# A planned transformer block on one core: the last quarter of the queries in two jobs, pooled PSUM banks, b2 on GpSimd, LN2's transposes by DMA

## The chip, the cores and the metric

The kernel runs on one core of one Trainium2 chip. A core has five engines with one in-order instruction queue each: TensorE (PE, matmuls), VectorE (DVE), ScalarE (ACT), GpSimd (POOL) and SyncE (SP, which here issues all DMAs). They wait for each other through semaphores. SBUF holds the working data, PSUM (eight banks of 128 x 512 fp32) what PE writes. The metric is the time of one execution on the device in microseconds (us), median of several runs.

## The reference

One pre-LN transformer block on 2048 tokens of width 1024, in bfloat16: 32 heads of 32 channels, full softmax attention, feed-forward width 3584, tanh GELU.

```python
q, k, v = qkv(x_norm @ wqkv)                       # x_norm = layernorm(x), 32 heads of 32
p = softmax(q @ k.T * 32 ** -0.5)                  # per head, 2048 x 2048
h = x + (p @ v) @ wo
out = h + gelu(layernorm(h) @ w1 + b1) @ w2 + b2   # (1024, 3584), (3584, 1024)
```

## The kernel before

**Attention.** The 2048 queries are handled in four chunks of 512 (`NCH`). A chunk runs through 16 pairs of heads (`p16`); for each pair eight rounds follow (`attention_round`). A round scores two blocks of 128 keys for two heads: four matmuls on four row groups of the array (`Att.qk`, L634), each 32 x 128 weights by 512 queries, into two "units" of two PSUM banks (three units, banks 0 to 5, take turns). ACT turns each unit into probabilities with one exp of 128 x 1024 elements (L643, 1024 of them in all). `pv_unit` (L654, L658) then accumulates values and row sums of one key block into bank 6, four narrow matmuls of 32 columns of weights side by side. After the last key block `finish` copies sums and values out (L666, L668), takes reciprocals (L673) and multiplies into `OT` (L680, in pieces of 128 queries for the very last pair, L677).

**Background.** PE has time left beside attention, and a list of "bg" tasks fills it, all through bank 7. Beside chunk 0 these are the rest of the q, k, v projections; beside chunk 1 to 3 the feed-forward part of the chunk before: `wo` (projection, x added by DVE, L719), `ln2`, `ffn1` and `ffn2`, with `late_q` (queries of a later chunk) between the second and third tile of LN2 for the first two of them. In the background a matmul of 128 columns of weights is given as four narrow ones on four column groups (`mm`, L439); four narrow matmuls of 512 columns take as long as one full one and are called a unit here. A group is what one bank takes: 8 units for wo, ffn1 and a late projection, 29 for ffn2, the first of them `two_row` times `b2t`, which adds twice b2 (the evacuation L782 halves the bank and adds h).

`ln2` takes statistics of a tile of 128 tokens on DVE, inverse roots on POOL (L492 to L498), normalises on DVE (L502), transposes eight 128 x 128 blocks on PE (L508) and copies the bank into `hnT` (L514 by DVE, L512 by ACT in the last chunk). `ffn1` adds b1 on the way out of PSUM (L748 by DVE, L751 by ACT in the last chunk), and GELU is x^2 (L754), a cubic (L756), tanh on ACT (L758) and a product (L760) into `gT`.

**The tail.** After chunk 3's attention nothing is left to run beside its own feed-forward part. It uses full matmuls (L443), all eight banks in turn, and a second set of ring buffers (`R2`) in the space of the keys and values. The weights come in blocks of 512 KB: w1 and wo through a ring of four slots (`w1r`), w2 through seven (`w2r`); two of w2's slots share their place with `hnT`, two with the late queries' input.

**The order.** Nothing is ordered at run time. `Graph.add` notes what each task reads and writes, and `Graph.schedule` simulates the five engines with fixed costs and writes one order per engine: PE takes qk first, pv when five are waiting (`PV_FORCE`) or no bg task is ready, else the earliest bg task (`pick_pe`); the other engines take the ready task of least `prio`, then the earliest. A bg task that needs bank 7 depends on the last reader of that bank. Semaphore waits are worked out from this order afterwards. At the very start PE runs 80 matmuls on `b2t` and `ident` (L798) when it has nothing else.

Of the kernel before, what the change touches and what calls it, by code (L numbers as in the profile page):

```python
# [27 lines left out]
class Task:  # L28
    __slots__ = ("eng", "fns", "occ", "lat", "deps", "prio", "kind", "mode", "left", "succ", "ready", "done",
                 "order", "inc", "flow", "value", "lane", "waits", "bytes", "hold")  # L30

    def __init__(self, eng, fns, occ, lat, prio, kind, mode):
# [14 lines left out]
        self.hold = None  # L47


class Graph:  # L50
# [7 lines left out]
    def __init__(self, n_lanes):  # L58
        self.tasks = []
        self.regions = {}  # L60
        self.n_lanes = n_lanes

# [35 lines left out]
    def schedule(self, pick_pe, switch=0.1, dma_rate=280.0, dma_lat=2.1, dma_issue=0.06):  # L98
# [13 lines left out]

        def release(t):
            t.ready = max([d.done - (d.lat if d.eng == t.eng == E.PE else 0.0) for d in t.deps], default=0.0)
            heapq.heappush(upcoming[t.eng], (t.ready, num[t], t))
            heapq.heappush(events, t.ready)
# [5 lines left out]
        while n < total:  # L122
# [5 lines left out]
            for e in self.ENGS:  # L128
                while free[e] <= now + 1e-9:
# [18 lines left out]
                    rd.remove(t)  # L148
                    start = now
                    if e == E.PE:  # L150
                        if state["mode"] != t.mode:
                            start += switch
                        state["mode"] = t.mode
# [16 lines left out]
                    heapq.heappush(events, free[e])  # L170
                    n += 1
                    for s in t.succ:
                        s.left -= 1
                        if s.left == 0:
                            release(s)
# [109 lines left out]
def build_kernel(nc, A_x, A_wqkv, A_wo, B_w1, B_b1, B_w2, B_b2, out):  # L285
# [51 lines left out]
    two_row, B_two = sb(top, "two_row", [P, P], BF)  # L337
# [91 lines left out]
    def pe(fns, occ, reads=(), writes=(), kind="bg", mode="full", prio=0, after=()):  # L429
        return gr.add(E.PE, fns, occ, 0.16, reads, writes, prio, kind, mode, after)  # L430

    def mm(bank, lhsT, rhs, start, stop, reads, narrow, cols=(0, 512)):
# [3 lines left out]
        if narrow:  # L436
            fns = []
            for j in range(4):
                fns.append(lambda p, j=j: p.matmul(psum[32 * j:32 * j + 32, bank, c0:c1], lhsT[:, 32 * j:32 * j + 32], rhs,  # L439
                                                   start=start, stop=stop, tile_position=(0, 32 * j), skip_group_check=True))  # L440
            pe(fns, occ, reads=reads, writes=[B_ps[bank]], mode="col")
        else:
            pe(lambda p: p.matmul(psum[:, bank, c0:c1], lhsT, rhs, start=start, stop=stop),  # L443
               occ, reads=reads, writes=[B_ps[bank]], mode="full")
# [18 lines left out]

    pool(lambda g: g.memset(ident[:], 0.0), 0.3, writes=[B_ident])
# [6 lines left out]
    pool(lambda g: g.memset(two_row[:], 0.0), 0.3, writes=[B_two])  # L471
    pool(lambda g: g.memset(two_row[0:1, :], 2.0), 0.3, reads=[B_two], writes=[B_two])
    pool(lambda g: g.memset(b2t[:], 0.0), 1.0, writes=[B_b2t])
# [32 lines left out]
    def transposes(src_ap, B_src, bank, dst_ap, B_dst, evac, prio):  # L506
        for dc in range(DC):
            pe(lambda p, dc=dc: p.transpose(psb[:, bank, dc * P:(dc + 1) * P], src_ap[:, dc * P:(dc + 1) * P], ident[:]),  # L508
               0.064, reads=[B_src, B_ident], writes=[B_ps[bank]], prio=prio)
        src = psb[:, bank, :].rearrange("p (dc t) -> p dc t", dc=DC)  # L510
        if evac == "act":
            act(lambda a: a.activation(dst_ap, src, ACT.Copy), 1024, reads=[B_ps[bank]], writes=[B_dst], prio=-1)  # L512
        else:
            dve(lambda v: v.tensor_copy(dst_ap, src), c_dve_ps(1024), reads=[B_ps[bank]], writes=[B_dst])  # L514

# [19 lines left out]
    def proj(which, g, tc, bank, evac, direct=False):  # L535

        blk, c = divmod(which * D + g * P, 512)
        for dc in range(DC):
            mm(bank, Wall[:, blk, dc, c:c + P], xnT[:, tc, dc, :], dc == 0, dc == DC - 1,
# [3 lines left out]
        if evac == "act":  # L543
            act(lambda a: a.activation(stg[:, s, :], psum[:, bank, :], ACT.Copy), 512,
                reads=[B_ps[bank]], writes=[B_stg[s]], prio=-1)
        else:
            dve(lambda v: v.tensor_copy(stg[:, s, :], psum[:, bank, :]), c_dve_ps(512), reads=[B_ps[bank]], writes=[B_stg[s]])  # L547
# [28 lines left out]
    def late_q(R, qc, gs):  # L576

        dma(R.xq[:, :, :], xd[qc - 1], P * 8192, reads=[B_xd[qc - 1]], writes=[R.B_xq], prio=0)
        for g2 in range(gs // 2, G // 2):
            s = wblock(R, A_wqkv[:, 256 * g2:256 * g2 + 256], 0)  # L580
            for k in range(2):
                g = 2 * g2 + k
                for dc in range(DC):
                    mm(7, R.w1[:, s, dc, k * P:k * P + P], R.xq[:, dc, :], dc == 0, dc == DC - 1,
                       [R.B_w1[s], R.B_xq], True)
                o = R.next("os", R.nos)
                dve(lambda v, o=o: v.tensor_copy(R.ost[:, o, :], psum[:, 7, :]), c_dve_ps(512),
                    reads=[B_ps[7]], writes=[R.B_ost[o]])
                dma(qd[g, qc], R.ost[:, o, :], P * 1024, reads=[R.B_ost[o]], writes=[B_qd[g][qc]], prio=0)

    def proj_v(tt, q, bank, evac):

        blk, c = divmod(256 * q, 512)
        blk += 4
        for k in range(2):
            tc, t4 = divmod(tt + k, 4)
            for dc in range(DC):
                mm(bank, xnT[:, tc, dc, t4 * P:(t4 + 1) * P], Wall[:, blk, dc, c:c + 256], dc == 0, dc == DC - 1,
                   B_W[blk][c // P:c // P + 2] + [B_xnTt[tc][t4]], True, cols=(256 * k, 256 * k + 256))
        dst = V[:, tt:tt + 2, 256 * q:256 * q + 256]  # L600
        src = psum[:, bank, :].rearrange("p (t c) -> p t c", t=2)
        wr = [B_V[4 * (tt + k) + q] for k in range(2)]
        if evac == "act":
            act(lambda a: a.activation(dst, src, ACT.Copy), 512, reads=[B_ps[bank]], writes=wr, prio=-1)
        else:
            dve(lambda v: v.tensor_copy(dst, src), c_dve_ps(512), reads=[B_ps[bank]], writes=wr)  # L606


    class Att:
# [9 lines left out]
        def qk(self, qc, units):  # L619

            fns, banks, rd, us = [], [], [], []
            for p16, kt in units:
                tc, k4 = divmod(kt, 4)
                half, i = divmod(k4, 2)
# [5 lines left out]
                for j in range(2):  # L630
                    r0 = 64 * half + 32 * j

                    def fn(p, j=j, r0=r0, u=u, p16=p16, tc=tc, i=i, qs=qs, pr=pr):
# [373 lines left out]
```

## Time and profile before

| | |
|---|---|
| median of 3 runs | 1203.92 us (1203.0 to 1205.25) |
| profiled execution, first to last instruction | 1417.9 us |
| mean granted TensorE clock in the profiled execution | 0.749 of full speed |
| busy PE / ACT / DVE / POOL | 1366.2 / 1085.3 / 673.2 / 37.9 us |
| 1024 exps (L643) | 989.2 us busy, 1025 ns each |
| last exp ends / last matmul ends | 1255.0 / 1415.0 us |

The profile is of one execution, which was longer than the timed ones; its page gives busy time by engine, its chain follows the work that ended last back from the end, its groups give the mean time of one instruction by line of the code, and its stages give busy time, granted clock and DMA use within a stretch. A busy PE counts pipelined matmuls, whose ends are modelled.

### The profile page before, as it was taken

What the parts mean: (1) busy time and instruction counts of PE and PEld (TensorE: products, weight loads), DVE (VectorE), ACT (ScalarE), POOL (GpSimd) and SP (SyncE); (2) the same over time, 40 slices, a digit from 0 to 9 for tenths busy, and PEclk for the clock granted to TensorE, in tenths of its full rate; (3) what the DMA queues carried; (4) which work ended last, traced back from release to release, by engine and by line L of the source; (5) the groups of instructions that cost most, each with busy time, mean ns of one, the idle gap of its engine ahead of it and who ended that gap; (6) DMA issues with size and microseconds to landing.
All of it is one profiled execution on the core that took longest, in us unless ns stands there. A gap on an engine that the chain in (4) does not pass through costs nothing.

```text
span 1417.9 us, 37847 instructions
## 1 busy us (share of the span) xinstructions
PE 1366.2 (96%) x17326; PEld 510.9 (36%) x17336; DVE 673.2 (47%) x1165; ACT 1085.3 (77%) x1189; POOL 37.9 (3%) x96
## 2 busy tenths in 40 slices
PE   8999999999999999999999999999999999978999
PEld 5544443433333333332333333333333333324333
DVE  7354444443546774223547762225677612245710
ACT  4778787878888888888888888888988888844500
POOL 2000000000100000000100000000000000001000
PEclk7777777777777777777777777777777777766777
DMA  6800000025343222303342230422323322202222
GB/s 165 224 2 13 28 13 14 13 72 156 101 122 101 76 69 72 124 16 98 107 124 71 83 98 16 124 71 63 107 73 98 102 66 85 87 0 75 74 93 71
DMA packets 165793, 112.29 MB, mean 79 GB/s; under 512 B 25345, under 2 KB 162817, under 8 KB 164866
## 3 DMA queue, kind: packets, MB, share of 16 engines
q1 hardware_dynamic: 165634, 109.87, 26.2%
q8 instruction: 136, 2.23, 0.7%
q14 instruction: 23, 0.19, 0.1%
HBM read 98.58 MB, written 11.27 MB: 77 GB/s over the span
## 4 chain that ended last, share of the span: by engine, by line
PE 91%; ACT 4%; DVE 3%; issue 1%; POOL 1%; DMA 0%; POOLq 0%; DVEq 0%
PE ps L439 48%; PE ps L654 17%; PE ps L634 12%; PE ps L443 10%; ACT PT L643 3%; PE ps L658 2%; PE ps L798 1%; ACT xnT L512 1%; DVE a_xh L748 1%; PE ps L508 1%; DVE V L606 0%; DVE stg L547 0%; DVE Osb L668 0%; DVE Dsb L666 0%; DMA a_w1r<-in_A_wqkv_dram 0%
## 5 line engine op out<-in xcount | busy, mean ns | idle before, releaser
L643 ACT ACTIVATE PT<-ps 128x1024 bf16<-128x1024 f32 x1024 | 989.2, 1025 | 180.5 <-PE ps L634 166.1
L654 PE MATMUL ps<-PT,V 128*32 128x512 bf16 x2048 | 383.4, 457 | 13.7 <-DVE V L606 6.2
L658 PE MATMUL ps<-PT,ones 128*32 128x512 bf16 x2048 | 384.8, 458 | 0.0
L439 PE MATMUL ps<-a_w2r,gT 128*32 128x512 bf16 x2688 | 241.9, 452 | 0.0
L634 PE MATMUL ps<-QT,KT 32*128 32x512 bf16 x2048 | 216.7, 414 | 7.4 <-ACT PT L643 7.3
L439 PE MATMUL ps<-a_hnT,a_w1r 128*32 128x512 bf16 x2688 | 215.2, 454 | 4.0 <-DVE a_xh L748 3.2
L654 PEld LDWEIGHTS ps<-PT,V 128*32 128x32 bf16 x2048 | 103.3, 104 | 143.9 <-issue 89.3
L634 PEld LDWEIGHTS ps<-QT,KT 32*128 32x128 bf16 x2048 | 51.5, 91 | 272.3 <-ACT PT L643 164.5
L439 PE MATMUL ps<-xnT,Wall 128*32 128x512 bf16 x1344 | 111.6, 453 | 7.0 <-ACT xnT L512 4.8
L439 PEld LDWEIGHTS ps<-a_w2r,gT 128*32 128x32 bf16 x2688 | 77.3, 109 | 112.0 <-issue 103.3
L673 DVE RECIPROCAL Dsb<-Dsb 128x128 f32<-128x128 f32 x128 | 115.1, 928 | 1.0
L439 PEld LDWEIGHTS ps<-a_hnT,a_w1r 128*32 128x32 bf16 x2688 | 70.6, 107 | 108.0 <-issue 71.4
L782 DVE SCALAR_TENSOR_TENSOR a_ost<-ps,hch 128x512 bf16<-128x512 f32 x24 | 16.6, 692 | 189.8 <-PE ps L439 189.7
L658 PEld LDWEIGHTS ps<-PT,ones 128*32 128x32 bf16 x2048 | 103.5, 104 | 6.6 <-issue 6.6
L748 DVE TENSOR_SCALAR a_xh<-ps,b1f 128x512 bf16<-128x512 f32 x84 | 63.1, 751 | 81.3 <-PE ps L439 80.2
L666 DVE COPY Dsb<-ps 64x512 f32<-64x512 f32 x64 | 44.4, 694 | 101.5 <-PE ps L658 100.1
L439 PE MATMUL ps<-Wall,xnT 128*32 128x256 bf16 x2048 | 83.8, 314 | 0.0
L547 DVE CAST stg<-ps 128x512 bf16<-128x512 f32 x40 | 27.5, 689 | 89.2 <-PE ps L439 89.2
L443 PE MATMUL ps<-a_hnT,b_w1r 128*128 128x512 bf16 x219 | 64.5, 470 | 2.1 <-ACT a_hnT L512 1.5
L439 PEld LDWEIGHTS ps<-Wall,xnT 128*32 128x32 bf16 x2048 | 57.6, 107 | 22.7 <-issue 11.3
L443 PE MATMUL ps<-a_w2r,gT 128*128 128x512 bf16 x219 | 64.1, 461 | 0.5
L439 PE MATMUL ps<-a_w1r,OT 128*32 128x512 bf16 x768 | 63.1, 453 | 0.8 <-DVE hch L719 0.5
(69 smaller groups left out, 875.5 us busy)
## 6 DMA issues: line engine op xcount, KB each, us to landing
a_w2r<-in_B_w_dram SPq DMA_DIRECT2D x56, 512.0 KB, 4.6
a_w1r<-in_B_w_dram SPq DMA_DIRECT2D x42, 512.0 KB, 3.9
a_w1r<-in_A_wo_dram SPq DMA_DIRECT2D x16, 512.0 KB, 4.7
QT<-q_scratch SPq DMA_DIRECT2D x60, 128.0 KB, 2.8
b_w1r<-in_B_w_dram SPq DMA_DIRECT2D x14, 512.0 KB, 3.8
a_w1r<-in_A_wqkv_dram SPq DMA_DIRECT2D x11, 512.0 KB, 5.1
xrb<-in_A_x_dram SPq DMA_DIRECT2D x16, 256.0 KB, 3.9
Wall<-in_A_wqkv_dram SPq DMA_DIRECT2D x16, 256.0 KB, 5.4
```

Source lines behind the costliest of these rows:

```text
L439: fns.append(lambda p, j=j: p.matmul(psum[32 * j:32 * j + 32, bank, c0:c1], lhsT[:, 32 * j:32 * j + 32], rhs, start=start, stop=stop, tile ...
L443: pe(lambda p: p.matmul(psum[:, bank, c0:c1], lhsT, rhs, start=start, stop=stop), occ, reads=reads, writes=[B_ps[bank]], mode="full")
L508: pe(lambda p, dc=dc: p.transpose(psb[:, bank, dc * P:(dc + 1) * P], src_ap[:, dc * P:(dc + 1) * P], ident[:]), 0.064, reads=[B_src, B_ide ...
L547: dve(lambda v: v.tensor_copy(stg[:, s, :], psum[:, bank, :]), c_dve_ps(512), reads=[B_ps[bank]], writes=[B_stg[s]])
L634: return p.matmul(psum[:, 2 * u + j, :], KT2[r0:r0 + 32, p16, tc, i, :], QT2[r0:r0 + 32, qs, pr, :], start=True, stop=True, tile_position= ...
L643: act(lambda a, u=u, s=s: a.activation(PT[:, s, :, :], psum[:, 2 * u:2 * u + 2, :], ACT.Exp, bias=0.0, scale=SCALE), 1024, reads=[B_ps[2 * ...
L654: fns.append(lambda p, j=j, h=h: p.matmul(psum[32 * j:32 * j + 32, bank, :], V[:, kt, 32 * h:32 * h + 32], PT[:, s, j, :], start=first, st ...
L658: fns.append(lambda p, j=j: p.matmul(psum[64 + 32 * j:96 + 32 * j, bank, :], ones32[:, :], PT[:, s, j, :], start=first, stop=last, tile_po ...
L666: dve(lambda v: v.tensor_copy(Dsb[64 * pr:64 * pr + 64, :], psum[64:128, bank, :]), c_dve_ps(512), reads=[B_ps[bank]], writes=B_Dsb[pr], p ...
L673: dve(lambda v, k=k: v.reciprocal(Dsb[:, 128 * k:128 * k + 128], Dsb[:, 128 * k:128 * k + 128]), 0.93, reads=[B_Dsb[0][k], B_Dsb[1][k]], w ...
L748: dve(lambda v, i=i, fc=fc, bank=bank: v.tensor_scalar(R.xh[:, i, :], psum[:, bank, :], b1f[:, fc:fc + 1], None, ALU.add), c_dve_ps(512), ...
L782: dve(lambda v, o=o, t4=t4, j=j, bank=bank: v.scalar_tensor_tensor(R.ost[:, o, :], psum[:, bank, :], 0.5, hch[:, t4, 512 * j:512 * j + 512 ...
```

## The change

Five things change. (1) Chunk 3 becomes two jobs of 256 queries. A unit of scores then holds two key blocks of 256 queries for two heads, so the exps stay 1024 of 128 x 1024, and qk, pv and ffn1 issue twice as many matmuls of half the width. The feed-forward part of the first half is a background job of its own, that of the second half the tail. (2) A bank is no longer written into a task: tasks form a `Group`, which gets a bank from a pool when its first matmul is picked. The pool holds bank 7, and banks 0 to 6 join as attention ends. A group may be picked when it is the earliest without a bank or when all that it depends on is done. Once the last exp is planned, an evacuation may go to ACT instead of DVE, whichever has less waiting (`alt`). (3) b2 is broadcast to 128 partitions by one DMA and added after the evacuation, on POOL in the background and on DVE in the tail; `two_row` and its matmuls go. (4) LN2's transposes of background jobs become one transposing DMA a tile on SP's queue; the tail keeps PE's. (5) The 80 matmuls at the start become 160 of 128 columns on `ident` alone.

```diff
+class Group:
+    def met(self, now):
+        if self.outside is None:
+            own = set(self.tasks)
+            self.outside = [d for d in {d for t in self.tasks for d in t.deps} if d not in own]
+        self.outside = [d for d in self.outside if d.done is None or d.done > now + 1e-9]
+        return not self.outside
...
+        def banks(now):
+            for x in list(self.joins):
+                if all(d.done is not None and d.done <= now + 1e-9 for d in x[1]):
+                    self.joins.remove(x)
+                    pool.append((max([d.done for d in x[1]], default=0.0), x[0], x[1]))
+            return [x for x in pool if x[0] <= now + 1e-9]
...
         def release(t):
+            if t.alt is not None and late():
+                e2, fns2, occ2, lat2 = t.alt
+                if load[e2] + occ2 < load[t.eng] + t.occ:
+                    t.eng, t.fns, t.occ, t.lat = e2, fns2, occ2, lat2
...
+                    if e == E.PE and t.grp is not None and t.grp.bank is None:
+                        x = min(banks(now))
+                        pool.remove(x)
+                        t.grp.bank = x[1]
+                        t.deps.update(x[2])
...
+    def dma_t(out_ap, in_ap, nbytes, reads=(), writes=(), prio=0):
+        return gr.add(E.SP, lambda s: s.dma_start_transpose(out_ap, in_ap), 0.06, 0.0, reads, writes, prio, nbytes=2 * nbytes)
...
+                for k in range(nk):
+                    for j in range(2):
+                        r0 = 64 * half + 32 * j
+                        def fn(p, j=j, r0=r0, u=u, p16=p16, tc=tc, i=i0 + k, qs=qs, pr=pr, k=k):
+                            return p.matmul(psum[:, 2 * u + j, nq * k:nq * k + nq], KT2[r0:r0 + 32, p16, tc, i, :],
+                                            QT2[r0:r0 + 32, qs, pr, q0:q0 + nq], start=True, stop=True, tile_position=(r0, 0))
...
+    def ln2(R, xbar, between=None, t4s=range(4)):
...
+            if xbar:
+                dma_t(R.hnT[:, :, t4 * P:(t4 + 1) * P], R.xb[:, s, :], P * 2048, reads=[R.B_xb[s]], writes=[R.B_hnT[t4]], prio=-2)
+            else:
+                transposes(R.xb[:, s, :], R.B_xb[s], gr.group(), R.hnT[:, :, t4 * P:(t4 + 1) * P], R.B_hnT[t4], "dve", 0)
...
+                    t = dve(lambda v, i=i, fc=fc, gp=gp, ps=ps: v.tensor_scalar(
+                        R.xh[:, i, ps], psum[:, gp.bank, ps], b1f[:, fc:fc + 1], None, ALU.add),
+                        c_dve_ps(nq), reads=[gp.buf, B_b1f], writes=[R.B_xh[i]])
+                    t.alt = (E.Activation, [lambda a, i=i, fc=fc, gp=gp, ps=ps: a.activation(
+                        R.xh[:, i, ps], psum[:, gp.bank, ps], ACT.Identity, bias=b1f[:, fc:fc + 1], scale=1.0)],
+                        c_act(nq, True), 0.14)
+                    reader(t, gp)
+                gelu(R, i, fcs, cols)
...
-                mm(bank, two_row[:, :], b2t[:, 512 * j:512 * j + 512], True, False, [B_two, B_b2t], len(banks) == 1)
...
+                add = (lambda e, i=i, o=o, j=j: e.tensor_tensor(
+                    R.ost[:, o, :], R.th[:, i, :], b2t[:, 512 * j:512 * j + 512], ALU.add))
+                if narrow:
+                    pool(add, 1.4, reads=[R.B_th[i], B_b2t], writes=[R.B_ost[o]])
+                else:
+                    dve(add, c_dve(512), reads=[R.B_th[i], B_b2t], writes=[R.B_ost[o]])
...
-    for k in range(80):
-        pe(lambda p: p.matmul(psum[:, 6, 0:256], ident[:, :], b2t[:, 0:256], start=True, stop=True), 0.12,
+    for k in range(160):
+        pe(lambda p: p.matmul(psum[:, 6, 0:128], ident[:, :], ident[:, :], start=True, stop=True), 0.06,
...
-    dma(b2t[0:1, :], B_b2.rearrange("(o d) -> o d", o=1), D * 2, writes=[B_b2t], prio=1)
+    dma(b2t[:, :], B_b2.partition_broadcast(P), P * D * 2, writes=[B_b2t], prio=1)
...
+    jobs = [(0, 0, 512), (1, 0, 512), (2, 0, 512), (3, 0, 256), (3, 256, 256)]
+    for n in range(1, len(jobs)):
+        qc, q0, nq = jobs[n - 1]
+        t4s = range(q0 // P, (q0 + nq) // P)
+        if n == 1:
             late_q(R1, 1, 2)
+        wo(R1, qc, R1, True, t4s)
+        ln2(R1, True, (lambda n=n: late_q(R1, n + 1, 0)) if n < 3 else None, t4s)
+        ffn1(R1, True, slice(q0, q0 + nq))
+        ffn2(R1, qc, True, t4s)
+        attention_chunk(*jobs[n])
         attention_flush()
+    for b in range(7):
+        gr.join(b, B_ps[b].w + B_ps[b].r)
...
+        free = bool(state["banks"](now))
         for t in rd:
+            if t.grp is not None and t.grp.bank is None and not (free and (t.grp is gr.groups[0] or t.grp.met(now))):
+                continue
...
+    gr.schedule(pick_pe, lambda: exps[-1].done is not None)
```

In the written order of the changed kernel, PE goes from the end of attention to ffn1 and ffn2 of the first half, then to Wo, the transposes, ffn1 and ffn2 of the second half; Wo of the first half stands before the last exps.

## The prediction

> **What bounds the kernel now.** I read the page first (busy shares, clock, chain), then the stages, then chain and timeline of the last 180 us, then the groups whose counts change.
>
> ```profile
> span 1417.9 us, 37847 instructions
> ...
> PE 1366.2 (96%) x17326; PEld 510.9 (36%) x17336; DVE 673.2 (47%) x1165; ACT 1085.3 (77%) x1189; POOL 37.9 (3%) x96
> ...
> PE 91%; ACT 4%; DVE 3%; issue 1%; POOL 1%; DMA 0%; POOLq 0%; DVEq 0%
> ```
>
> PE bounds this execution, which is 214 us longer than the median of the timed runs. The stages say why:
>
> ```profile
> 20.00:1236.00 1216.00, 1185.46 (x16539) 434.26 (x16531) 585.31 (x1001) 1023.80 (x1104) 24.29 (x57) 0.75 0.27 80
> 1236.00:1255.00 19.00, 14.92 (x127) 3.44 (x123) 1.38 (x2) 18.50 (x20) 0.00 (x0) 0.66 0.00 0
> 1255.00:1418.00 163.00, 150.11 (x541) 60.90 (x550) 72.28 (x130) 37.88 (x61) 6.38 (x16) 0.73 0.22 68
> 1271.40:1284.00 12.60, 3.96 (x32) 3.30 (x34) 7.35 (x20) 3.98 (x4) 6.38 (x16) 0.58 0.00 1
> 40.00:44.00 4.00, 4.00 (x84) 2.17 (x80) 3.18 (x8) 2.85 (x4) 0.00 (x0) 0.75 1.10 221
> 388.00:392.00 4.00, 4.00 (x60) 1.50 (x52) 3.14 (x5) 3.39 (x4) 0.00 (x0) 0.75 1.09 282
> 732.00:736.00 4.00, 3.96 (x52) 1.56 (x48) 3.20 (x5) 3.91 (x5) 0.00 (x0) 0.75 1.06 333
> ```
>
> Columns: busy PE, weight loads, DVE, ACT, POOL; granted clock; DMA share; GB/s. The clock was 0.75. Until 1236 PE is 97% busy; ACT, with 1024 us of work, is not far below. After 1255 attention is over and the last chunk's feed-forward part runs alone (the tail), with PE nearly idle for 12.6 us in LN2. The last rows are bursts in which the DMA engines are full: 221 to 333 GB/s.
>
> ```profile
> 1238.44 13.86 ACT PT L643 x15
> ...
> 1256.81 14.26 PE ps L443 x50
> ...
> 1284.09 15.63 PE ps L443 x49
> ...
> 1299.88 14.03 PE ps L443 x49
> ...
> 1314.06 14.03 PE ps L443 x49
> ...
> 1415.06 0.69 DVE b_ost L782
> ```
>
> The chain: when PE has no background left, ACT sets the pace; the tail is Wo (1256.8 to 1271.4), LN2 to 1284.1, then 456 matmuls to 1415.0. Later pieces start 14.18 us apart for 50 matmuls: 0.284 us per unit (one full matmul of 512 columns, or four narrow ones side by side).
>
> ```profile
> 142.23 2.46 PE L439 MATMUL ps<-Wall,xnT 128*32 128x256 bf16 x64
> ...
> 1238.44 16.60 ACT L643 ACTIVATE PT<-ps 128x1024 bf16<-128x1024 f32 x18 [0.22 <-PE ps L634]
> ```
>
> From the timeline: 64 narrow matmuls of 256 columns (8 units) take 2.46 us with the last one's drain, so half-width costs nothing per column at this clock; 18 exps in a row take 0.922 each.
>
> ```profile
> L508 PE MATMUL ps<-ident,a_xb 128*128 128x128 bf16 x96 | 8.4, 237 | 0.0
> L439 PE MATMUL ps<-b2t,two_row 128*32 128x512 bf16 x96 | 10.6, 434 | 2.5 <-DVE a_ost L782 2.5
> ```
>
> These groups leave the background: 8.4 us of transposes and 96 narrow b2 matmuls, which are 24 units.
>
> **The change part by part, in the profiled execution (1417.9).** The order of instructions shows that the planner does not move the first half's feed-forward work under attention: chunk 2's work fills all of chunk 3, only Wo of the first half (32 units) fits before the last exp, and its ffn1 and ffn2 (112 units each) come after it, ahead of Wo, LN2, ffn1 and ffn2 of the second half. So the tail shrinks little.
>
> Attention, PE-paced: b2 rows -24 x 0.284 = -6.8; transposes -8.4; Wo of the first half +32 units for 7 that move back, +7.1. LN2's transposes by DMA: today the last tile goes from normalised (1007.06) to transposed (1010.58) in 3.5 us; no row shows a transposing DMA. Landings bound it: 2.3 us (128 KB of x) and 7.6 (1 MB out of SBUF), nearest 3.9 (256 KB of x, the same bytes); I take 4. In chunks 0 and 1 the late Q projections (71 and 62 units, over 17 us) follow Wo and hide even 7.6; in chunk 2 and at the tail nothing does. There PE's queue stands at ffn1's first matmul, with qk and pv behind it and ACT waiting for those: +1, between -1 and +8. On SP, each transpose waits for its tile, and loads of x, w1 and QT queue behind it; w1 and QT are ring buffers requested blocks ahead, so nothing is added. Copies out of pv's bank are twice as many and half as wide in chunk 3: today PE and its weight loads wait at most 16.7 us for 64 of them, 0.26 each, so 16 more pairs (32 copies) add +1, +4 at most. Half-wide qk and pv (384 units in chunk 3): 0 by the row above, +10 at most. Sum: -6.1.
>
> Nothing at the start, +1.3 at most: 150 warm matmuls (128 columns, 0.08 each by the 160 ns of today's 256) begin 1.2 us earlier, since b2t's memset is gone, and end near 13.5 against 12.4; but the second pair of tiles follows after 8 of them, not 18 wide ones. The b2 add on GpSimd (28 of 32): bounds 0.69 (DVE's row of the same shape) and a few us; it hides behind the next 28-unit group (8 us), and costs that excess if longer. GpSimd's port to SBUF is no bound by any row here. The last add, on DVE, is exposed: +0.7.
>
> Tail from the last exp's end (1255.0), today 162.9. After: ffn1 of the first half, 105.5 units left plus 2 of pv, 30.5; its ffn2, 31.8; Wo 9.1; LN2 for two tiles instead of four, 8.2 against 12.7 (last add, two statistics, aggregate, POOL's four, normalise, transposes and copy, by today's rows); PE's slow first stretch after that gap 1.5, as today (15.63 against 14.03); 224 units 63.6; last evacuation, add, DMA 3.6. Sum 148.3: -14.6. Total 1417.9 - 6.1 - 14.6 = 1397.
>
> **From there to the timed runs.** They take 0.849 of this span, so PE ran faster there, 0.241 per unit if all scales. Three things change. First, attention: 1204 - 20 of start - 141 of tail leaves 1043, while ACT alone needs 1024 x 0.922 + 84 tanh x 0.54 (0.63 less the overlap) + some 20 of copies = 1009. ACT is within 3% of its floor, so most of the 6.1 is hidden: -1, between 0 and -5. Second, DVE: a tile of ffn1 needs 0.42 + 0.68 + 0.68, and 11 of 28 half-wide evacuations at about 0.5 (half to whole of 0.75), 30.3 for 14 tiles; with the last softmax copies and reciprocals (3.3) and the start (2.5) the first half's last tile is ready 36.5 after PE begins, while PE could use it at 33.7. Third, weights: a half job reads the whole of w1 and w2 for half the columns. In ffn2's second pass seven 512 KB blocks at 333 GB/s (1.57 each, first 4.6 after release) land up to 2.2 us late, in both jobs. Tail then: today 162.9 - 507 x 0.043 = 141.1; after: 36.5 - 1.2 (begun before the last exp ends) + 20.2 + 2.2 + 7.7 + 9.7 + 54.0 + 2.2 + 3.6 = 134.9, -6.2. 1203.9 - 6.2 - 1 = **1197**.
>
> Two rules of the skill speak against parts of this. The DMA row above gave 4 us for 256 KB; "Advanced Engine Details and Errata", section X-Bar Transpose, has transposes nearly as fast as copies, but its section DGE: Hardware vs Software calls a hardware queue's transpose efficiency worse than a software queue's; no run here shows it, and the sum is unchanged by the first and one or two us longer by the second. The granted clock here was 0.75; "TensorE: Matmul & The Clock Gate", Part 1, says one busy core never trips the current limiter, which this execution contradicts; if it held in the timed runs, the full-clock rival below would be the case.
>
> **The rivals.**
> PE-bound all through (timed clock near 0.88): speaks for it the scaling of nearly everything by 0.849; against, ACT's 3%. All gains scale: 0.849 x 20.7 = 17.6, 1186.
> Full clock, no gain: 0.213 per unit. Tail today 162.9 - 507 x 0.071 = 126.9; after, DVE still 36.5, blocks 3.4 late twice: 127.8. With attention's -1: 1204.
> Slower, transposing DMA: at ffn1's first matmul in chunk 2 and the tail. With 12 us from issue to landing, chunk 2 loses 8 less the three exps already scored (2.8), the tail 8: +13, 1210. It decides from about 8.5 us. For: no row prices it, and SP, which sends all loads, must send it too; against: all landings up to 512 KB have medians under 6.2 us, those of 256 KB 3.9 and 5.4.
> Slower, weight stream: in the tail, at ffn1's later blocks and ffn2's second pass. At 221 GB/s a block takes 2.4 to 2.6 us against PE's 1.93 per eight units: about +5 and +6 in each job less what DVE hides, +19, 1216. It decides below some 255 GB/s. For: the tail asks 270 GB/s where today 81 to 86 flow; against: w1 and w2 bursts reach 282 and 333.
>
> **How the numbers follow.** Forecast 0.42 (1192 to 1201); PE-bound 0.20; full clock 0.14, half of it within 0.2%; transposes 0.12; weights 0.12. 0.2% (2.4 us) is about what a measurement can tell. Faster: 0.42 + 0.20 + 0.02 = 0.64; same 0.07; slower 0.05 + 0.24 = 0.29. The range runs from below the PE-bound case, 1182, to between the two slower ones, 1214.
>
> **What would show it.** Last exp to the end near 135 to 148 us (by clock) and PE stopped less than 10 us there before Wo; no b2 matmuls; transposing DMAs landing in about 4 us, ffn1's first matmuls not waiting for them; ACT's exps unchanged. I am wrong if PE waits on w1 or w2 in the tail, if ffn1 waits for hnT by more than 3 us, or if half-wide qk and pv take longer per column: were their second weight loads (0.10 us) all exposed, 384 units would add 38 us of PE work, of which ACT hides most.

## The result and the profile after

The changed kernel takes 1211.39 us (median of 4 runs, 1208.28 to 1213.0) against 1203.93 for the kernel before beside it: ratio 1.0059, 95% interval 1.0043 to 1.0076. Measured again later (e15): 1.0083, 1.0069 to 1.0098. It is 7 to 10 us slower where 6.9 us less were forecast.

The only profile of before so far had a granted clock of 0.75. A second one, of the unchanged kernel (e0), has 0.99, as all timed runs here have (0.975 to 0.997), so it is the one to compare. Lines of its page (span, busy time of each engine, shares of the chain):

```profile
span 1200.6 us, 37847 instructions
...
PE 1128.3 (94%) x17326; PEld 465.2 (39%) x17336; DVE 668.5 (56%) x1165; ACT 1059.3 (88%) x1189; POOL 38.3 (3%) x96
...
PE 74%; ACT 11%; DVE 11%; DMA 1%; issue 1%; POOL 1%; SPq 0%; POOLq 0%; DVEq 0%
```

and two windows of it, attention from 20 us to the end of the last exp, then the tail (columns: window, length, busy PE, weight loads, DVE, ACT, POOL, clock, DMA share, GB/s):

```profile
20.00:1070.80 1050.80, 995.25 (x16618) 399.47 (x16610) 582.42 (x1001) 1015.63 (x1123) 24.82 (x58) 1.00 0.31 92
1070.80:1200.70 129.90, 117.32 (x541) 53.56 (x550) 71.09 (x130) 37.96 (x61) 6.46 (x16) 0.95 0.28 85
```

The same lines of the page of the changed kernel:

```profile
span 1206.1 us, 43520 instructions
...
PE 1121.5 (93%) x20064; PEld 510.8 (42%) x20064; DVE 674.2 (56%) x1208; ACT 1061.5 (88%) x1202; POOL 69.9 (6%) x121
...
PE 66%; ACT 19%; DVE 9%; DMA 4%; issue 2%; SPq 0%; POOL 0%; POOLq 0%; DVEq 0%
```

and its two windows (the first starts at its first exp):

```profile
24.90:1080.20 1055.30, 990.28 (x18032) 418.66 (x18032) 585.40 (x1035) 1015.78 (x1121) 55.05 (x88) 0.99 0.36 100
1080.20:1206.20 126.00, 109.52 (x1704) 74.03 (x1696) 71.00 (x129) 38.85 (x73) 7.71 (x12) 0.97 0.70 206
```

Between these two executions PE does 6.8 us less work and the kernel is 5.5 us longer. The tail is 3.8 us shorter, so attention lost more than that. ACT runs 1024 exps in every kernel of this study, 256 for each chunk, so the starts of the nth exp in the timelines are marks that can be laid side by side. From exp 256 to exp 768 attention works on chunks 1 and 2, with the background of chunks 0 and 1 beside it; from exp 768 on it works on chunk 3, beside the background of chunk 2. All times in us, from one profile each:

| kernel | to exp 256 | 256 to 768 | 768 to last exp's end | tail | ratio to before |
|---|---|---|---|---|---|
| e0 before | 298.6 | 515.2 | 257.1 | 129.8 | 1 |
| changed | 301.8 | 517.1 | 261.3 | 126.0 | 1.0059 |
| e15 changed, again | 303.5 | 518.5 | 260.3 | 127.0 | 1.0083 |
| e1 one job | 301.6 | 519.2 | 257.4 | 128.5 | 1.0048 |
| e2 PE transposes | 299.7 | 514.4 | 257.1 | 130.0 | 1.0031 |
| e3 b2 on DVE | 302.0 | 518.9 | 262.0 | 127.6 | 1.0051 |
| e4 chunk ends filled | 299.8 | 518.7 | 258.1 | 127.6 | 1.0044 |
| e7 DMA transposes late only | 302.7 | 514.6 | 258.5 | 127.0 | 1.0004 |
| e8 as e7, two fills | 303.9 | 514.8 | 256.3 | 132.9 | 1.0055 |
| e9 as e7, one job | 301.5 | 516.1 | 256.1 | 128.5 | 0.9999 |
| e12 changed, early Q weights | 302.1 | 516.5 | 261.1 | 126.7 | 1.0057 |
| e14 as e7, tail fill | 301.3 | 514.3 | 259.4 | 122.6 | 1.0006 |
| e5 before + DMA transposes | 298.5 | 516.2 | 258.5 | 127.7 | 1.0033 |
| e6 before + tail fill | 300.0 | 515.8 | 256.6 | 129.2 | 0.9985 |
| e10 before + late DMA, tail fill | 300.6 | 515.3 | 257.1 | 128.5 | 0.9984 |
| e11 before + b2 on GpSimd | 302.3 | 515.1 | 256.2 | 126.4 | 1.0008 |
| e13 before + early Q weights | 299.0 | 514.5 | 256.8 | 128.6 | 0.9996 |
| e16 before + new warm-up | 300.9 | 516.0 | 256.1 | 129.8 | 1.0007 |
| e17 before + e10 + e13 | 300.9 | 514.5 | 256.4 | 126.0 | 0.9972 |

One profile differs from the next of the same kernel by 1 to 2 us in a stage (see the two of the changed kernel), so single rows decide little and groups of rows more. A profile is also of one run, and not always of a typical one: those of e2, e5, e14 and the first of the changed kernel are of runs 3.7, 5.5, 3.6 and 3.1 us below their kernel's median, that of e3 is 3.7 above. The ratios come from 4 to 12 runs each, with intervals of 1 to 2 thousandths to each side.

### The profile page after: what moved, and what is told of

The parts are those of the page before. It is cut to its first block, busy times and chain, and to the rows that moved or that the text cites. A ratio compares the mean times of both kernels' runs of the same rounds, so it can differ in the third digit from the quotient of the medians.

```text
span 1206.1 us, 43520 instructions
## 1 busy us (share of the span) xinstructions
PE 1121.5 (93%) x20064; PEld 510.8 (42%) x20064; DVE 674.2 (56%) x1208; ACT 1061.5 (88%) x1202; POOL 69.9 (6%) x121
## 4 chain that ended last, share of the span: by engine, by line
PE 66%; ACT 19%; DVE 9%; DMA 4%; issue 2%; SPq 0%; POOL 0%; POOLq 0%; DVEq 0%
PE ps L518 40%; ACT PT L736 17%; PE ps L752 11%; PE ps L726 9%; PE ps L522 4%; DVE a_xh L874 3%; ACT xnT L594 1%; DMA a_w1r<-in_A_wqkv_dram 1%; DMA q_scratch<-stg 1%; PE ps L922 1%; DVE a_uu L847 1%; DVE gT L853 1%; DMA QT<-q_scratch 1%; DVE Osb L769 1%; DVE stg L631 1%
## 5 line engine op out<-in xcount | busy, mean ns | idle before, releaser
L752 PE MATMUL ps<-PT,V 128*32 128x512 bf16 (+1 forms) x2560 | 316.9, 340 | 14.6 <-DVE Osb L769 5.6
L756 PE MATMUL ps<-PT,ones 128*32 128x512 bf16 (+1 forms) x2560 | 317.1, 340 | 0.5 <-issue 0.5
L726 PE MATMUL ps<-QT,KT 32*128 32x512 bf16 (+1 forms) x2560 | 203.7, 342 | 23.2 <-ACT PT L736 19.8
L518 PE MATMUL ps<-a_hnT,a_w1r 128*32 128x512 bf16 (+1 forms) x3584 | 202.3, 356 | 17.0 <-DVE a_xh L874 9.2
L767 DVE COPY Dsb<-ps 64x512 f32<-64x512 f32 (+1 forms) x80 | 47.0, 587 | 131.4 <-PE ps L756 129.7
L874 DVE TENSOR_SCALAR a_xh<-ps,b1f 128x512 bf16<-128x512 f32 (+1 forms) x95 | 68.1, 717 | 39.0 <-PE ps L518 35.6
L903 POOL TENSOR_TENSOR a_ost<-a_th,b2t 128x512 bf16<-128x512 f32 x28 | 32.8, 1173 | 639.1 <-DVE a_th L900 639.1
L849 ACT ACTIVATE a_th<-a_uu 128x512 f32<-128x512 bf16 x98 | 61.9, 634 | 9.0 <-DVE a_uu L847 8.5
L853 DVE SCALAR_TENSOR_TENSOR gT<-a_th,a_xh 128x512 bf16<-128x512 f32 x98 | 65.9, 673 | 3.7 <-ACT a_th L849 3.4
L847 DVE SCALAR_TENSOR_TENSOR a_uu<-a_sq,a_xh 128x512 bf16<-128x512 bf16 x98 | 66.6, 682 | 1.6
```

Source lines behind the costliest of these rows:

```text
L726: return p.matmul(psum[:, 2 * u + j, nq * k:nq * k + nq], KT2[r0:r0 + 32, p16, tc, i, :], QT2[r0:r0 + 32, qs, pr, q0:q0 + nq], start=True, ...
L752: fns.append(lambda p, j=j, h=h, kt=kt, cols=cols, st=st, sp=sp: p.matmul(psum[32 * j:32 * j + 32, bank, 0:nq], V[:, kt, 32 * h:32 * h + 3 ...
L756: fns.append(lambda p, j=j, cols=cols, st=st, sp=sp: p.matmul(psum[64 + 32 * j:96 + 32 * j, bank, 0:nq], ones32[:, :], PT[:, s, j, cols], ...
L767: dve(lambda v: v.tensor_copy(Dsb[64 * pr:64 * pr + 64, 0:nq], psum[64:128, bank, 0:nq]), c_dve_ps(nq), reads=[B_ps[bank]], writes=B_Dsb[p ...
L847: dve(lambda v: v.scalar_tensor_tensor(R.uu[:, i, :], R.sq[:, i, :], C2, R.xh[:, i, :], ALU.add, ALU.mult), c_dve(512), reads=[R.B_sq[i], ...
L849: act(lambda a: a.activation(R.th[:, i, :], R.uu[:, i, :], ACT.Tanh, bias=0.0, scale=K2 / 2), 512, reads=[R.B_uu[i]], writes=[R.B_th[i]], ...
```

## The experiments

Two theories at first. A: the split of the last chunk loses, since its tail reads w1 and w2 twice and DVE paces its ffn1. B: the edits of the background lose under attention.

**e0**, the kernel before, unchanged.

> The kernel before, unchanged, for a profile at about the clock of the timed runs (its only profile so far had 0.75; the changed kernel's had 0.99). If the loss of 7.5 us lies in the tail, the time from the last exp to the end is near 121 us here against the 128.7 of the changed kernel, and the last exp ends near 1077 in both. If it lies under attention, the tail is 127 to 129 us here as well and the last exp ends near 1070.

Last exp's end 1070.8 here, 1080.2 in the changed kernel; tails 129.8 and 126.0. The loss lies under attention, and the tail gains.

**e1**, one job for the last chunk:

```diff
-    jobs = [(0, 0, 512), (1, 0, 512), (2, 0, 512), (3, 0, 256), (3, 256, 256)]
+    jobs = [(0, 0, 512), (1, 0, 512), (2, 0, 512), (3, 0, 512)]
```

> The changed kernel with the last chunk in one job of 512 columns again; pooled banks, b2 on GpSimd and transposing DMAs stay. Theory A (the split loses: its tail reads w1 and w2 twice and its ffn1 is paced by DVE): 1198 to 1203, at or below the kernel before. Theory B (the background edits lose under attention and the split is about neutral): 1209 to 1213, as the changed kernel.

1.0048 (1.0031 to 1.0064), 1207.7 us, between A's band and B's, nearer to B's: undoing the split gives back little, and most of the loss stays.

**e2**, LN2's transposes on TensorE again:

```diff
-        ln2(R1, True, (lambda n=n: ...
+        ln2(R1, False, (lambda n=n: ...
```

> The changed kernel with the transposes of LN2 on TensorE again in the background; split, GpSimd add and pooled banks stay. Theory A (split): 1210 to 1214, the changed kernel's time or up to 3 us more, since PE gets 56 more transposes and 7 more copies back. Theory B (the transposing DMAs stall SP and PE): 1203 to 1206, and ffn1's first matmul of each chunk starts earlier after the last normalise.

1.0031 (1.0021 to 1.0041), 1206.7 us: between the two. In its profile attention is back at the pace of before (514.4 and 257.1) and the tail is not shorter any more. But with no transposing DMA left in it, this version is still slower than the kernel before.

**e3**, the b2 add on DVE everywhere (`if narrow: pool(add, ...)` taken out).

> The changed kernel with the b2 add of all 32 tiles on DVE; everything else stays. The add takes 1.17 us on GpSimd and 0.69 on DVE, and GpSimd is otherwise idle there. If GpSimd's add costs nothing where it stands (both theories as I hold them): the changed kernel's time within 2 us, 1209 to 1213. If it slows DVE or ACT by its traffic, or holds buffers, 1204 to 1207.

1.0051 (1.0033 to 1.0070), 1208.8 us: GpSimd's add is not the cause. In the changed kernel it takes what its group shows, off the chain of the profile, and the transposing DMAs land as the second line (of the DMA issues) says:

```profile
L903 POOL TENSOR_TENSOR a_ost<-a_th,b2t 128x512 bf16<-128x512 f32 x28 | 32.8, 1173 | 639.1 <-DVE a_th L900 639.1
...
a_hnT<-a_xb SPq DMA_TRANSPOSE x14, 4.0
```

**e5 and e7**, the transposing DMAs alone, and those of the late chunks alone:

```diff
 # e5, in the kernel before, ln2:
+            if len(banks) == 1:
+                gr.add(E.SP, lambda q, t4=t4, s=s: q.dma_start_transpose(R.hnT[...], R.xb[...]), ...)
+                continue
 # e7, in the changed kernel:
-        ln2(R1, True, (lambda n=n: ...
+        ln2(R1, n >= 3, (lambda n=n: ...
```

> The kernel before with one part alone: LN2's transposes of the three background chunks by transposing DMAs on SP, everything else as before. Theory A (the transposing DMAs lose: SP's queue, the landing at ffn1's first matmul, and the clock after both): ratio 1.002 to 1.006, with late exps near exps 576 to 608 and 832 as in the changed kernel. Theory B (they are hidden, and the loss needs the other parts): ratio 0.997 to 1.001.

> The changed kernel with transposing DMAs only for chunk 2 and the first half of the last chunk; chunks 0 and 1 transpose on TensorE. The prediction's step (late Q hides the landing in chunks 0 and 1, nothing hides it in chunk 2): the loss is all here, ratio as the changed kernel, 1.005 to 1.007, and the exps fall behind only near exp 832. If the transposing DMAs lose in chunks 0 and 1 as well, by holding the late Q weights back on SP's queue: 1.003 to 1.005, between the version without them (1.003) and the changed kernel (1.006), and no step near exps 320 to 350 and 576 to 608.

e5: 1.0033 (1.0022 to 1.0045): one part alone makes before some 4 us slower; its profile, of its fastest run, does not contain that loss. e7: 1.0004 (0.9990 to 1.0017): without the eight transposing DMAs of chunks 0 and 1 the changed kernel is level with before. This is the reverse of what the prediction held, and against both of the numbers that I gave: these eight cost as much as the whole change loses. The table points the same way. From exp 256 to 768 the seven profiles with early transposing DMAs take 516.2 to 519.2 (mean 517.9), the other twelve 514.3 to 516.1 (515.1): 2.8 us, of some 7 in the timed runs. In chunk 3 and the tail together the DMA is no loss: e7 385.5, e2 387.1, e0 386.9.

One result does not fit a simple account. e2 has no transposing DMA at all and was at 1.0031; e7 has the six late ones and was at 1.0004, and the intervals part. In this kernel the six look like a gain of some 3 us, in the kernel before (e10 below, chunk 2 alone) like nothing. So the other parts together may cost some 4 us where TensorE transposes. No run says which part.

What happens there shows in SP's queue. SP around late Q of chunk 1, kernel before (start, duration, issue):

```profile
587.80 1.53 SPq L460 DMA_DIRECT2D a_w1r<-in_A_wqkv_dram  x2
589.38 1.68 SPq L460 DMA_DIRECT2D a_xr<-in_A_x_dram  x1
591.11 1.92 SPq L460 DMA_DIRECT2D a_w1r<-in_A_wqkv_dram  x2
```

Changed kernel, and its waits of TensorE between 570 and 612 us:

```profile
589.68 1.96 SPq L539 DMA_DIRECT2D a_w1r<-in_A_wqkv_dram  x2
592.01 0.84 SPq L539 DMA_DIRECT2D a_xr<-in_A_x_dram  x1
592.92 1.84 SPq L544 DMA_TRANSPOSE a_hnT<-a_xb  x1
594.86 2.00 SPq L539 DMA_DIRECT2D a_w1r<-in_A_wqkv_dram  x2
```

```profile
PE ps L518 <- DMA a_w1r<-in_A_wqkv_dram: 1.9, 1, 1.9
```

A transposing DMA holds SP for 1.24 to 2.67 us in this profile, here for 1.84, and late Q's second pair of weight blocks goes out 5.2 us after the first instead of 3.3. TensorE stands 1.9 us for these weights (0.8 us in chunk 0's turn; 2.4 and 1.0 in e15), which it does at neither place in e0, e2 and e7; there the transposes of the first two tiles are TensorE's work in just this gap. Late Q itself is not later by it: its first matmul comes 2.8 us after Wo's last here and 5.4 in e0. If the stop costs time, it is through the qk and pv that stand behind it in TensorE's order.

**e12 and e13**, late Q's weights into three idle slots of w2's ring, in the changed kernel and, as control, in the one before:

```diff
-            s = wblock(R, A_wqkv[:, 256 * g2:256 * g2 + 256], 0)
+            s = g2 % 3
+            dma(R.w2[:, s, :, :].rearrange("p q (h c) -> p (q h) c", h=2), A_wqkv[...], ...)
```

> The changed kernel with late Q's weight blocks loaded into three idle slots of w2's ring, long before Wo ends, instead of w1's ring, where SP sends them behind the transposing DMAs; all transposes of LN2 in the background stay on the DMA. Theory A (the loss in chunks 0 and 1 is late Q waiting for these weights): TensorE's waits of 0.8 and 1.9 us on them go, ratio 0.999 to 1.003, near the 1.0004 of the version whose chunks 0 and 1 transpose on TensorE. Theory B (it is the landing, or the clock, by itself): 1.004 to 1.007.

> The same edit in the kernel before, as a control: there no transposing DMA stands ahead of these weights, and its trace shows no wait of TensorE on them. Both theories: 0.998 to 1.001. If the edit is a gain by itself here too, the gain of the run above says little on the transposing DMAs.

e12: 1.0057 (1.0044 to 1.0070) beside 1.0083 for the unchanged one on the same chip; e13: 0.9996. The waits on the weights are gone, but the time is far from 1.0004: theory A of that run explains a third at most, and nothing if the changed kernel's first measurement (1.0059) is taken. The order shows another cost: late Q, free of Wo, now starts at 552.0, before Wo, and ends at 605.4, the last tile lands at 614.9, and ffn1 starts at 616.0. TensorE has no background for 10 us, and the clock falls to 0.5 from 615 on. The wait for weights has become a wait for the landing that late Q used to hide. So that the early transposing DMAs cost time is shown, by e7 and by e5; that the queue is part of the way in which they do is likely, not shown. The hole that the transposes and their copies leave behind Wo may be the rest, but no run isolates it.

**e4, e6, e8, e14**: unused matmuls in the gaps of TensorE (their results are not used):

```diff
+    for k in range(n):
+        pe(lambda p: p.matmul(psum[:, bank, 0:256], ident[:, :], b2t[:, 0:256], start=True, stop=True), 0.12,
+           reads=[B_ident, B_b2t], writes=[...], kind="warm", after=last)
```

> The changed kernel with 40 extra matmuls of 128x256 (8.6 units, 1.8 us at full clock, results unused) in the idle places of TensorE after the last ffn2 group of the first and the second background job, where the profile shows TensorE idle 35% of 15 us, and a granted clock of 0.5 right after it (from 563.5 and 822.9 us). Theory A (the emptied background costs through the clock): no 0.5 stretch near 563 and 823, time 1 to 4 us below the changed kernel, ratio to the kernel before 1.002 to 1.005. Theory B (ACT sets the pace there and the half-clock stretches are hidden): ratio unchanged, 1.005 to 1.007.

> The kernel before with 64 unused matmuls of 128x256 in TensorE's gap at LN2 of the tail, where it now stands idle 5.8 us, then 0.6, 1.0 and 1.5, and where the granted clock is 0.5 for 13.65 us afterwards: the first 60 matmuls of ffn1 take 15.83 us there instead of 12.8. If the idle gap causes the half clock: 2 to 4 us less than before, ratio 0.997 to 0.998. If not: 0 to 1 us more.

> The version with transposing DMAs only for chunk 2 and the first half of the last chunk (ratio 1.0004), and unused matmuls of 128x256 in TensorE's gaps at LN2: 16 before ffn1 of chunk 2, 48 in the tail. Theory (each idle gap of TensorE brings a stretch at half clock, and the next work bound by TensorE pays about half of it): the tail's 6.83 us at half clock after LN2 shrink to 3.41 or nothing and the 6.83 us near 859 too, 2 to 4 us less, ratio 0.997 to 0.999, below the kernel before. Rival (half clock there is hidden by ACT and DVE): 1.000 to 1.001.

> Transposing DMAs for chunk 2 and the first half of the last chunk alone (1.0004), with 48 unused matmuls in the tail's gap at LN2, and none in chunk 2, where 16 had moved the order and left TensorE 5.3 us for the landing of hnT after attention. If the idle gap's half clock costs in the tail: 0.997 to 0.9995, and no 0.5 stretch after LN2. If not: 1.000 to 1.001.

e6: 0.9985 (0.9974 to 0.9996), 1.8 us faster than before, by adding work. The kernel before in LN2's gap of the tail, windows of 4 us (the clock is the third figure from the end):

```profile
1084.00:1088.00 4.00, 0.00 (x0) 0.00 (x0) 3.96 (x11) 0.00 (x0) 1.80 (x7) 0.98 0.00 0
1088.00:1092.00 4.00, 2.03 (x18) 1.77 (x19) 2.56 (x9) 1.55 (x2) 3.58 (x9) 0.50 0.00 0
1092.00:1096.00 4.00, 1.93 (x16) 1.40 (x14) 0.55 (x1) 2.44 (x3) 1.09 (x2) 0.50 0.01 2
1096.00:1100.00 4.00, 3.57 (x9) 1.50 (x11) 0.00 (x0) 0.34 (x1) 0.00 (x0) 0.50 0.00 0
```

and with the gap filled (e6):

```profile
1088.00:1092.00 4.00, 4.00 (x39) 3.60 (x37) 4.00 (x12) 0.00 (x0) 3.23 (x10) 1.00 0.00 0
1092.00:1096.00 4.00, 3.21 (x40) 2.56 (x38) 1.44 (x6) 2.85 (x3) 3.15 (x7) 1.00 0.03 6
1096.00:1100.00 4.00, 2.68 (x13) 1.18 (x14) 0.15 (x1) 1.02 (x1) 0.00 (x0) 0.75 0.00 0
```

TensorE was idle for 5.8 us, then ran at half clock for 13.65, and ffn1's first 49 matmuls took 13.24 us where the next 49 took 10.74. Filled, 3.41 us at half clock are left.

e4: 1.0044 (1.0028 to 1.0059) against 1.0059 and 1.0083: in the expected direction; only against the second do the intervals part. One of the two half-clock stretches that it aimed at is gone (823), the other is still there (565). Inconclusive, and the fill was larger than I said: back to back its matmuls start 0.109 us apart, so 40 are 4.4 us and not 1.8. e8: 1.0055 where 0.998 was expected. My edit was at fault: the fill's reader stands in DVE's queue ahead of LN2, so chunk 2's tiles were normalised up to 868.6 instead of 857.5 and ffn1 started at 871.8 instead of 862.2; chunk 3's background slid, the first half's LN2 came after attention, and TensorE then stood 5.3 us for hnT. That is the place and the mechanism of the rival "Slower, transposing DMA", but in this kernel, not in the changed one. e14, without that fill: no half clock after LN2, and a tail of 122.6 in its profile, yet 1.0006 (0.9992 to 1.0019) in the timed runs, no gain over e7. The profile is of the fastest of its twelve runs, so the short tail is not a typical one. Why the tail fill helps before and not here stays open.

**e9**, e7 with one job.

> Transposing DMAs only for chunk 2, and the last chunk in one job of 512 columns: tells the worth of the split without the early transposes. If the split is worth the 3.8 us that the profiles' tails differ by: 3 to 4 us more than with it, ratio 1.003 to 1.004. If the split is worth about nothing, as the two versions with all transposing DMAs suggested (1.0059 with it, 1.0048 without): 0.999 to 1.001.

0.9999 (0.9989 to 1.0008) against e7's 1.0004 (0.9990 to 1.0017): the split is worth nothing that can be measured.

**e10, e11, e16**, parts alone in the kernel before: e10 with the transposing DMA for chunk 2 (`qc == 2`) and e6's fill; e11 with b2 on GpSimd; e16 with 160 warm matmuls of 128 columns.

> The kernel before with transposing DMAs for chunk 2 alone, and the 64 unused matmuls in the tail's gap at LN2 (these alone: 0.9985). If transposing DMAs cost only where late Q's weights stand behind them on SP: 0.996 to 0.999. If they cost in chunk 2 as well (ffn1 waiting for the landing): 1.000 to 1.002.

> The kernel before with one part alone: b2 added on GpSimd (on DVE in the tail) instead of 64 narrow and 8 full matmul rows. My step: 24 of these units leave attention, which ACT's pace hides in all but 0 to 1 us, and the last add on DVE is exposed for 0.7 us: ratio 0.999 to 1.001. If an emptier TensorE costs through the clock: 1.001 to 1.003.

> The kernel before with the changed kernel's 160 narrow warm matmuls at the start (128 columns from ident, instead of 80 of 256 columns from b2t), nothing else. The prediction has 0 for this (1.3 at most): ratio 0.999 to 1.001. The profiles of all versions with it have their first exp 0.8 to 3.5 us later than the kernel before and exp 32 some 1 us later; if this edit is the cause, 1.0005 to 1.002, with the first transposes after 12 us instead of 10.9.

e10: 0.9984 (0.9975 to 0.9993), as e6 alone: in the kernel before, chunk 2's transposing DMA is neutral. e11: 1.0008 (0.9996 to 1.0021) and e16: 1.0007 (0.9996 to 1.0018): neither is told from no change.

**e15**, the changed kernel again, and **e17**, e10 and e13 together.

> The changed kernel once more, unchanged, beside the three above: 1.0043 to 1.0076 as before, and a second profile of it. It tells whether the half-clock stretch near 864 us (6.83 us) and TensorE's waits at 338 and 594 us are there each time.

> The kernel before with the three edits that did not lose: late Q's weights in w2's idle slots (0.9996), transposing DMAs for chunk 2 alone with the tail's gap filled (0.9984). If they add up: 0.9970 to 0.9990, the fastest so far; if late Q's earlier weights give nothing beside the others: 0.998 to 0.999.

e15: 1.0083, partly above the expected band; its profile has both waits on late Q's weights and half clock from 863.0 for 10.24 us. e17: 0.9972 (0.9959 to 0.9984), 1200.13 us: faster than both kernels, with one of the change's parts, the transposing DMA, at one of its four places.

## Why the prediction was wrong

6.9 us less were forecast and 7 to 10 us more measured. Two terms of the sum carry this. The tail's -6.2 was not there: without the split the kernel is no slower. And the 0 for what the transposing DMAs of chunks 0 and 1 do was 7 us or more in this kernel.

**The way to the timed runs.** The step "0.241 per unit if all scales" fails. It spread one execution's clock over the others. At the clock of the timed runs 49 units take 10.74 us, 0.219 each, and the tail of before is 129.8, not 141.1. The rival "Full clock, no gain" (0.14) had its condition met: it gave tails of 126.9 and 127.8, measured are 129.8 and 126.0. The Trainium skill's page "TensorE: Matmul & The Clock Gate", Part 1, with which the prediction argued, says that one busy core does not trip the current limiter. All timed runs here agree with it. The prediction said that the execution at 0.75 contradicts it, but what held the clock there no run shows.

**The tail.** Its terms, predicted and measured, on the chain of the changed kernel:

```profile
1061.70 15.74 ACT PT L736 x17
...
1086.57 3.68 PE ps L518 x128
1090.25 1.17 issue
...
1109.78 5.88 DMA a_w2r<-in_B_w_dram
1115.70 19.39 PE ps L518 x356
1135.10 7.03 PE ps L522 x32
...
1149.58 14.58 PE ps L522 x112
1164.17 6.41 DMA b_w1r<-in_B_w_dram
1170.63 30.53 PE ps L522 x172
...
1203.24 0.69 DVE b_ost L903
```

and of the kernel before (e0):

```profile
1072.42 9.19 PE ps L443 x42
...
1096.43 13.24 PE ps L443 x49
...
1109.72 10.74 PE ps L443 x49
...
1168.84 6.16 DMA a_w2r<-in_B_w_dram
```

ffn1 and ffn2 of the first half 54.9 after the last exp (35.3 + 20.2 + 2.2 predicted; ffn1 is paced as foreseen, DVE 90 to 98% busy and TensorE stopping 0.4 to 1.2 us after each 128 matmuls); Wo 7.0 (7.7); LN2 7.4 (9.7); then 51.6 for the second half (54.0 + 2.2); 4.9 at the end (3.6). A DMA piece of the chain is not a stop of that length, as work was queued behind it. The waits after 1070 us give the real stops. TensorE's weight loads stood 3.5 us for blocks of w2 and w1 in all, against the 4.4 predicted, in the first half's ffn2 and the second half's ffn1 (us in total, times, longest):

```profile
PEld ps L518 <- DMA a_w2r<-in_B_w_dram: 1.8, 2, 1.5
PEld ps L522 <- DMA b_w1r<-in_B_w_dram: 1.7, 3, 0.9
```

Its matmuls stood for less, 1.1 us in the first half (their group, below) and 0.9 in the second. So the rival "weight stream" did not decide.

```profile
L518 PE MATMUL ps<-a_w2r,gT 128*32 128x512 bf16 x3136 | 220.1, 381 | 2.4 <-DMA a_w2r<-in_B_w_dram 1.1
```

The tail shrank by 3.8 and 2.8 us in two profiles. But chunk 3 grew by 4.1 and 3.2: the sum from exp 768 to the end is 387.2 in both, 386.9 in e0. Over all versions without a fill it is 387.4 with the split (6 profiles) and 385.3 without (7): not -6.2, but nothing or a little loss, as e9 against e7 and e1 against the changed kernel say too. The step took chunk 3 as no longer for the first half's Wo and LN2 and the half-wide matmuls, because ACT has the pace there ("-1, between 0 and -5"). With the split, chunk 3 takes 260.0 us on average over the versions without a fill, without it 256.9. Which of these does it no run isolates; e2, at 257.1, has them all, with TensorE's transposes in place of the DMAs.

**The transposing DMAs.** The size was right: landings of 4 us were taken, the median is 4.0. Late Q hides the landing in chunks 0 and 1, as said: the last tile lands at 606.7, ffn1 starts at 621.7. ffn1 of chunk 2 does not wait longer either: from the last normalised tile to its first matmul it is 5.3 us, in e0 4.7. The step that fails is the next one, on SP: "w1 and QT are ring buffers requested blocks ahead, so nothing is added". Late Q's blocks are not: they are requested when Wo gives up their slots, and TensorE has its next use for them at once. The term was 0; the profiles give 2.8 us, e5 alone 4 us, and the changed kernel against e7 some 7 us or more (1.0059 and 1.0083 against 1.0004). How much of this is the queue stays open, as e12 showed: a third at most went with the wait for the weights. For chunk 2 and the tail the step had +1, from -1 to +8; e10 leaves it near 0, e7 against e2 below that.

**The clock, which the prediction does not have.** Chunk 2's ffn1 in the changed kernel, windows of 4 us:

```profile
856.00:860.00 4.00, 2.58 (x56) 0.84 (x56) 2.37 (x7) 4.00 (x6) 1.72 (x4) 1.00 0.93 213
860.00:864.00 4.00, 2.02 (x48) 0.60 (x40) 0.00 (x0) 4.00 (x5) 0.00 (x0) 0.99 1.33 190
864.00:868.00 4.00, 3.19 (x32) 0.94 (x36) 0.00 (x0) 1.40 (x3) 0.00 (x0) 0.50 0.27 69
868.00:872.00 4.00, 4.00 (x64) 1.50 (x60) 2.03 (x5) 2.71 (x3) 0.00 (x0) 0.66 0.02 4
```

and with TensorE transposing (e2):

```profile
852.00:856.00 4.00, 1.93 (x36) 0.92 (x30) 3.44 (x8) 4.00 (x5) 1.24 (x3) 0.99 0.69 167
856.00:860.00 4.00, 3.53 (x60) 1.86 (x64) 0.77 (x2) 3.42 (x5) 0.00 (x0) 0.59 0.25 68
860.00:864.00 4.00, 3.69 (x88) 1.81 (x84) 1.18 (x2) 3.98 (x5) 0.00 (x0) 1.00 0.01 2
```

While TensorE waits for hnT (landing 864.7) it is half busy, ACT is at its pace, and nothing seems lost. Then ffn1 and qk start at half clock for 6.83 us and ACT falls to 1.40 of 4.00: between exps 800 and 832 the changed kernel loses 5.0 us on e0. Over the versions this step goes roughly with the half-clock stretch there: -0.5 to 1.0 us where there is none (e4, e6, e9, e11, e13, e16), 0.1 to 3.4 with 3.41 us, 3.5, 3.6 and 5.0 with 6.83 (but 0.6 in e10, and a gain in e8, whose ffn1 came later), 4.7 and 5.2 with 10.24. That is no proof. The wait for hnT is not much longer where time is lost (from the last normalised tile to ffn1 5.3 us in the changed kernel, 4.7 in e0, 4.7 in e7, which loses 3.5), but the missing transposes may act in another way. Nor do the timed runs' clocks order the kernels: the median is 0.979 to 0.984 in the changed kernel, e1, e3, e5 and e12, but 0.991 in e4 and e2, which are slower than before too, and 0.984 and 0.985 in e9 and e11, which are level.

**What was right.** The b2 add on GpSimd is hidden (1.17 us each; e3, e11), the warm-up costs nothing that can be measured (e16), and taking background groups out of order changes nothing: with the head group alone allowed, the planner writes the same order of instructions on every engine. What stays open: the versions built on the changed kernel reach exp 256 at 301.8 on average and those built on the one before at 300.1, before any transposing DMA has run. e11 (302.3) and e16 (300.9) carry a part each, but e0, e6 and e10, whose edits act later, alone spread from 298.6 to 300.6.

## What to carry to other kernels

Work taken off an engine is a gain only where that engine has the pace, and a hole left on TensorE can cost twice where the clock falls behind it, as in LN2's gap that e6 fills: look at what is next in the hole, not only at the sum of busy time. When a step moves to a DMA, write down what the issuing queue sends just behind it and when the receiver of that has its next work; a ring of buffers says nothing where the slots come free only at that moment. Prices of parts need not add up: taking out all transposing DMAs (e2) gave back less than taking out eight of them (e7). Before scaling a profile to timed runs, find one at their clock.

## What the runs showed of the hardware

The clock of TensorE moved in steps of 3.41 us between 1 and 0.5 in all 19 profiles at the clock of the timed runs. Laying a grid of 3.413 us on the clock's changes and taking TensorE's busy share of each step: at full clock, some 6280 steps were at least 64% busy and none was followed by half clock; of 194 below that 93 were, and of the 17 below 40% all. At half clock, a step under 70% busy was never followed by full clock (33), one of 90% or more in 81 of 83. So an engine that is 60% busy, waiting for ACT, can lose half its clock, and gets it back only by being nearly full for a step. The Trainium skill, "TensorE: Matmul & The Clock Gate", Part 1, has the two rates and the length of the window, and an idle window as what brings the half rate; these traces agree on the length and show that a window far from idle is enough.

Unused matmuls in a gap made a kernel faster (e6), and a DMA that transposes 256 KB held the queue that issues it for 1.24 to 2.67 us (median 1.27) in the changed kernel's profile, where plain ones of x (128 KB) took 0.33 to 1.98 (median 0.34).
